# Turning the column order of the MoE matmuls' moving operand and result

## The chip, the cores and the metric

The kernel runs on one core of one Trainium2 chip. The metric is the device time of one execution in microseconds (us). The reported time of a kernel is the median of several executions; the profile is one further execution of its own.

## The reference

The reference has two stages. The first is a set attention over four batches of 12480 tokens with 128 channels: 32 inducing vectors attend to all tokens of their batch, and then every token attends to the 32 vectors that came out. The second is a dense feed-forward layer (called MoE in the code, though it has no routing) on all 49920 tokens.

```python
def mab(q, kv):
    s = scale * (q @ kv.transpose(0, 2, 1))
    s = s - s.max(-1, keepdims=True)
    a = np.exp(s)
    a /= a.sum(-1, keepdims=True) + 1e-09
    return a @ kv
h = mab(I, x)            # 32 vectors per batch
x = mab(x, h)            # 49920 tokens x 128
hidden = x @ w_in        # 128 -> 2048
g = hidden * (1.0 / (1.0 + np.exp(-1.702 * hidden)))
out = g @ w_out          # 2048 -> 128
```

The weights arrive as 64-bit numbers, which the kernel turns into float32 on the chip.

## The kernel before

**Layout.** Channels or hidden units lie on the 128 partitions and tokens along the free axis, so a matmul has a 128x128 block of weights as its stationary operand, 512 tokens as its moving operand, and a 128x512 result in one bank of PSUM. The tokens are worked through in blocks of 512 (some left-over blocks are 384 wide, made of two parts of 192). The hidden layer has 2048 / 128 = 16 chunks; two neighbouring chunks form one step, so a block has 8 steps, and all 98 blocks have 784 steps.

**The first MoE matmul** (`firsts`, the matmul at line 491). The second attention ends in a product with 32 vectors `h`, and the first MoE layer is a product too, so the kernel forms `h @ w_in` once per batch (`hw`) and multiplies the attention weights with it. The 32 weights of each token stand four times above one another in `st`, as a rounded upper part and a rest, against upper part and rest of `hw`; so one matmul with 128 rows gives the product at nearly full precision. Both operands are of the type float32r, a rounded float32 that TensorE takes in one go. The result goes to the two halves `ph[:, 0]` and `ph[:, 1]` of a PSUM tile of two banks; there are two such tiles.

**The activation** (`gelus`, line 515, on ScalarE) reads both halves of `ph` in one instruction and writes `g` in float32. `g` is then split into a rounded part `hi` (either by ScalarE from `ph` a second time, line 531, or by VectorE from `g`, line 538) and a rest `lo = g - hi` (VectorE, line 547).

**The second MoE matmul** (`seconds`, lines 605 to 607) adds three products per chunk into `pso`: `wl` with `hi`, `wh` with `lo`, and `wh` with `hi`, where `wh` and `wl` are the rounded part and the rest of `w_out`. Sixteen chunks make 48 matmuls into one bank, of which the first starts and the last ends the sum. The first 12 steps of the kernel are the exception: there `w_out` is not split yet, and one full float32 matmul per chunk (`whole`, line 591, weights `wf`) takes `g` as it is. A block whose early chunks went that way has its later chunks added by lines 605 to 607 into the same `pso`. When the sum is complete, `out` copies it to `ob` (lines 567 and 570) and SyncE's queue stores it.

**Buffers.** `hi`, `lo`, `st` and `hw` come from `spaced`, which makes each buffer 8 elements longer than its data (`STEP = 8`). There are six buffers each of `hi` and `lo`, three of `g`, two of `ph` and two of `pso`.

**Order.** Nothing is scheduled on the chip. When the program is built, the class `Plan` simulates all engines with a cost for each `Job` and writes out one fixed order of instructions per engine. Its cost for a float32r matmul is `2.5 + 0.447 * w` nanoseconds for `w` columns (lines 497 and 610). The attention of the next batch is woven in between the MoE steps of the current one: its matmuls (lines 300, 308, 319, 821) go to TensorE between MoE matmuls, and its exponentials, transposes and sums to ScalarE and VectorE. TensorE thus has one list of instructions, in which the four turned lines (491, 605, 606, 607) make up most of the entries. Each matmul is preceded by a weight load that shows on its own row of the profile (PEld).

**What waits for what around the changed lines.** Line 491 waits for `st` and `hw` (DMA), and for its `ph` buffer to be read by lines 515 and 531. Lines 605 to 607 wait for `hi` and `lo`, and at the first chunk for the `pso` buffer. Line 515 waits for the second half of `ph`, and line 567 or 570 for the last matmul of a block. All these waits are on whole instructions.

Of the kernel before, what the change touches and what calls it, by code (L numbers as in the profile page):

```python
# [17 lines left out]
P = 128  # L18
# [216 lines left out]
def set_attention_then_moe(ctx: ExitStack, tc, xT, x, indT, w_in, w_out, outT):  # L235
# [211 lines left out]
    def new_st(name):  # L447
        return Unit(NG, parts=G if len(name) == 3 else 2 * RG * G)
# [4 lines left out]
    def tokens(i):  # L453
        return sum(p[2] for p in work[steps[i][0]][1])

    def late(least, most):
        return lambda: most if ahead() >= AHEAD else least
# [16 lines left out]
    def firsts():  # L474
        for i in range(n):
            bi, k = steps[i]
            key, of = work[bi]
            if key not in st_units:
                st_units[key] = new_st(key)
            for b, _, _, _ in of:  # L480
                for c in range(G):
                    h_units.setdefault((b, c), Unit(uses_hw[b], parts=G))
            stu = st_units[key]
            hwu = [h_units[b, 2 * k // 4] for b, _, _, _ in of]

            def emit(i=i, k=k, of=of, stu=stu, hwu=hwu):
                st, ph = stu.ap, phs[i].ap
                for c in range(2):
                    ch = 2 * k + c
                    for (b, at, w, _), u in zip(of, hwu):  # L490
                        pe_.matmul(  # L491
                            ph[:, c, at:at + w], u.ap[:, ch % 4 * P:(ch % 4 + 1) * P],
                            st[:, at:at + w], start=True, stop=True,
                        )
                counts["F"] = i + 1

            one_ = 2.5 + 0.447 * tokens(i)
            yield Job("PE", emit, 2 * one_, 2 * one_ + 200, [stu, *hwu], takes=[(r_ph, phs[i])], rank=(1, i), slack=late(0, 800))
# [63 lines left out]
    def out(bi, pso):  # L562
        w = sum(p[2] for p in work[bi][1])
        ob = Unit(len(work[bi][1]))

        def by_act():
            act.copy(ob.ap[:, 0:w], pso.ap[:, 0:w])  # L567

        def by_dve():
            dve.tensor_copy(ob.ap[:, 0:w], pso.ap[:, 0:w])  # L570

        yield [
            Job("ACT", by_act, *on_act(w), [pso], [], [(r_ob, ob)], rank=(0, bi)),
            Job("DVE", by_dve, *on_dve(w), [pso], [], [(r_ob, ob)], rank=(0, bi)),
        ]
        yield from store(bi, ob)

    def seconds():
        psos = {}
        for i, (bi, k) in enumerate(steps):  # L580
            w = tokens(i)
            if k == 0:
                psos[bi] = Unit(parts=NCH)
            pso = psos[bi]
            for c in range(2):
                ch = 2 * k + c

                join = {"joins": [pso]} if ch else {"takes": [(r_po, pso)]}

                def whole(i=i, c=c, ch=ch, w=w, pso=pso):  # L590
                    pe_.matmul(  # L591
                        pso.ap[:, 0:w], wf[:, ch * P:(ch + 1) * P], gs[i].ap[:, c, 0:w],
                        start=(ch == 0), stop=(ch == NCH - 1),
                    )
                    counts["S"] += 1

                if i < plain:
                    occ = 4 * (1 + 0.4185 * w)
                    yield Job("PE", whole, occ, occ + 200, [gs[i], wf_units[ch // G]], rank=(2, i), **join)
                    continue  # L600

                def emit(i=i, c=c, ch=ch, w=w, pso=pso):
                    o = pso.ap[:, 0:w]
                    hi, lo = his[i].ap[:, c, 0:w], los[i].ap[:, c, 0:w]
                    pe_.matmul(o, wl[:, ch, :], hi, start=(ch == 0), stop=False)  # L605
                    pe_.matmul(o, wh[:, ch, :], lo, start=False, stop=False)  # L606
                    pe_.matmul(o, wh[:, ch, :], hi, start=False, stop=(ch == NCH - 1))  # L607
                    counts["S"] += 1

                occ = 3 * (2.5 + 0.447 * w)  # L610
                yield Job(
                    "PE", emit, occ, occ + 200, [his[i], los[i], w_out_units[ch // G]], rank=(2, i), **join,
                )
            if k == NG - 1:
                plan.spawn(out(bi, pso))
# [1049 lines left out]
```

## Time and profile before

| what | value |
|---|---|
| time, median of 3 executions | 1584.58 us (1583.19 to 1584.76) |
| time of the profiled execution | 1583.06 us |
| span of the profiled execution, first to last instruction | 1581.3 us |
| mean granted TensorE clock | 1.000 |
| TensorE busy | 1566.8 us (99%) |
| weight loads busy | 1222.0 us (77%) |
| VectorE busy | 1336.9 us (85%) |
| ScalarE busy | 1323.7 us (84%) |
| DMA, mean over the span | 79 GB/s |

The span is the part that the profile sees; 1583.06 - 1581.3 = 1.8 us of the execution's own time lie outside it. In a row of the profile the line number is that of the kernel, then come the engine, the operation, the names of output and inputs, the shapes, and the count of instructions; behind the bar stand the busy time in us, the mean duration of one in ns, and the idle time of the engine just before such instructions with what ended it. Matmuls are pipelined: the record of one begins before the record of its predecessor ends, so the duration of one record is longer than its share of the time. The share is read from the distance between the starts of two neighbouring matmuls, called the pitch in what follows. The type in a matmul's row says f32 for float32 and float32r alike.

### The profile page before, as it was taken

Reading aid. Unit: us, or ns where it says so; the run is one execution under the profiler, and the core shown is the slowest. Engines: PE = TensorE matmul, PEld = TensorE weight load, DVE = VectorE, ACT = ScalarE, POOL = GpSimd, SP = SyncE. Lnnn points to the kernel's source line nnn. Section 1 sums busy time; section 2 is a strip of 40 time slices with the busy share of each in tenths; the row PEclk is TensorE's granted clock in tenths of the full one; section 3 lists DMA queues with packets and bytes.
Section 4 is the critical chain, followed back from the end, with each engine's and each line's share of the span. In section 5 each row is a group of like instructions: output and inputs, shape, how many; then the busy total and the mean of one; then the engine's idle time right before and its main releaser. Section 6 shows DMA issues by size and latency. Waiting matters only on the chain.

```text
span 1581.3 us, 21430 instructions
## 1 busy us (share of the span) xinstructions
PE 1566.8 (99%) x7693; PEld 1222.0 (77%) x7693; DVE 1336.9 (85%) x1616; ACT 1323.7 (84%) x1502; POOL 0.7 (0%) x6
## 2 busy tenths in 40 slices
PE   8999999999999999999999999999999999999999
PEld 6467777777877887777777887787788878888887
DVE  6999888888888888879888888798898898888886
ACT  5898888788887888878888888798888888887876
POOL 0000000000000000000000000000000000000000
PEclk9999999999999999999999999999999999999999
DMA  7354253430123406342014427220101101111100
GB/s 270 139 190 87 80 102 80 136 113 28 52 97 125 87 27 124 70 150 93 27 41 146 117 54 142 76 72 27 41 26 42 38 29 42 37 36 32 41 27 21
DMA packets 84474, 125.06 MB, mean 79 GB/s; under 512 B 12113, under 2 KB 51601, under 8 KB 78993
## 3 DMA queue, kind: packets, MB, share of 16 engines
q1 hardware_dynamic: 84368, 123.69, 28.4%
q8 instruction: 62, 1.02, 0.3%
q14 instruction: 44, 0.35, 0.1%
HBM read 70.43 MB, written 25.56 MB: 61 GB/s over the span
## 4 chain that ended last, share of the span: by engine, by line
PE 61%; ACT 0%; issue 0%
PE ph L491 15%; PE pso L605 15%; PE pso L607 15%; PE pso L606 15%; PE pa L308 1%; PE pa L319 1%; PE pa L300 0%; PE pa L821 0%; ACT g L515 0%; ACT e L746 0%; ACT L515 0%; ACT ob L567 0%; PE pa L331 0%; ACT e_last L746 0%; PE pa L332 0%
## 5 line engine op out<-in xcount | busy, mean ns | idle before, releaser
L547 DVE TENSOR_TENSOR lo<-g,hi 128x1024 fp32r<-128x1024 f32 (+1 forms) x772 | 929.8, 1215 | 192.4 <-ACT hi L531 180.8
L515 ACT ACTIVATE g<-ph 128x1024 f32<-128x1024 f32 (+1 forms) x784 | 804.3, 1032 | 220.0 <-PE ph L491 94.0
L605 PE MATMUL pso<-hi,wl 128*128 128x512 f32 (+1 forms) x1544 | 607.8, 394 | 0.0
L606 PE MATMUL pso<-lo,wh 128*128 128x512 f32 (+1 forms) x1544 | 606.6, 393 | 0.5 <-DVE lo L547 0.5
L607 PE MATMUL pso<-hi,wh 128*128 128x512 f32 (+1 forms) x1544 | 606.9, 393 | 0.0
L531 ACT ACTIVATE hi<-ph 128x1024 fp32r<-128x1024 f32 (+1 forms) x460 | 474.6, 1034 | 4.6 <-PE pso L607 4.3
L491 PE MATMUL ph<-st,hw 128*128 128x512 f32 x1536 | 467.5, 400 | 4.1 <-ACT hi L531 1.6
L491 PEld LDWEIGHTS ph<-st,hw 128*128 128x128 f32 x1536 | 282.4, 188 | 97.5 <-ACT g L515 10.8
L605 PEld LDWEIGHTS pso<-hi,wl 128*128 128x128 f32 x1544 | 290.1, 188 | 70.4 <-issue 3.6
L606 PEld LDWEIGHTS pso<-lo,wh 128*128 128x128 f32 x1544 | 290.1, 188 | 67.7 <-DVE lo L547 1.4
L607 PEld LDWEIGHTS pso<-hi,wh 128*128 128x128 f32 x1544 | 290.0, 188 | 66.4
L538 DVE CAST hi<-g 128x1024 fp32r<-128x1024 f32 (+1 forms) x312 | 210.6, 681 | 13.5 <-ACT g L515 9.6
L567 ACT COPY ob<-pso 128x512 f32<-128x512 f32 (+1 forms) x70 | 41.7, 595 | 9.8 <-PE pso L607 9.5
L570 DVE COPY ob<-pso 128x512 f32<-128x512 f32 x28 | 19.2, 684 | 8.0 <-PE pso L607 7.8
L300 PE MATMUL pa<-xt,indT_sb 128*32 128x512 f32 x192 | 23.7, 599 | 1.3 <-DMA xt<-in_xT 1.2
L591 PE MATMUL pso<-g,wf 128*128 128x512 f32 x48 | 23.1, 594 | 0.0
L308 PE MATMUL pa<-xt,hT 128*32 128x512 f32 x184 | 22.9, 599 | 0.0
L319 PEld LDWEIGHTS pa<-xn,t 128*32 128x32 f32 (+1 forms) x594 | 15.6, 110 | 4.4 <-issue 3.6
L319 PE MATMUL pa<-xn,t 128*32 128x128 f32 (+1 forms) x594 | 18.8, 274 | 0.0
L970 DVE TENSOR_TENSOR t<-t,two 128x512 f32<-128x512 f32 (+1 forms) x27 | 16.7, 618 | 1.3 <-ACT two L959 1.0
L871 DVE STREAM_TRANSPOSE e<-pa 128x512 f32<-128x512 f32 x23 | 15.9, 702 | 0.5 <-PE pa L308 0.4
L954 DVE STREAM_TRANSPOSE t<-e 128x512 f32<-128x512 f32 x23 | 16.2, 705 | 0.1
(169 smaller groups left out, 421.2 us busy)
## 6 DMA issues: line engine op xcount, KB each, us to landing
xt<-in_xT SPq DMA_DIRECT2D x42, 1024.0 KB, 6.3
out_T<-ob SPq DMA_DIRECT2D x96, 256.0 KB, 2.0
xn<-in_x SPq DMA_DIRECT2D x72, 256.0 KB, 6.9
st<-two SPq DMA_DIRECT2D x184, 64.0 KB, 2.0
st<-t SPq DMA_DIRECT2D x184, 64.0 KB, 2.0
hw<-t SPq DMA_DIRECT2D x48, 64.0 KB, 3.2
raw<-in_w_in SPq DMA_DIRECT2D x4, 512.0 KB, 6.9
raw<-in_w_out SPq DMA_DIRECT2D x4, 512.0 KB, 5.0
```

Source lines behind the costliest of these rows:

```text
L300: pe_.matmul(pa[32 * j:32 * j + 32, 0:w], indT_sb, xg[:, j], start=True, stop=True)
L308: pe_.matmul(pa[32 * j:32 * j + 32, 0:w], hT[:, 0:M], x[:, j * w:(j + 1) * w], start=True, stop=True,)
L319: pe_.matmul(pa[32 * j:32 * j + 32, 0:P], aT[0:q, kk, :], xn[0:q, kk] if second is None or kk < BLK // 2 else second[0:q, kk - BLK // 2], ...
L491: pe_.matmul(ph[:, c, at:at + w], u.ap[:, ch % 4 * P:(ch % 4 + 1) * P], st[:, at:at + w], start=True, stop=True,)
L515: act.activation(gs[i].ap[:, :, 0:w], phs[i].ap[:, :, 0:w], AF.Gelu_apprx_sigmoid)
L531: act.activation(his[i].ap[:, :, 0:w], phs[i].ap[:, :, 0:w], AF.Gelu_apprx_sigmoid)
L538: dve.tensor_copy(his[i].ap[:, :, 0:w], gs[i].ap[:, :, 0:w])
L547: dve.tensor_sub(los[i].ap[:, :, 0:w], gs[i].ap[:, :, 0:w], his[i].ap[:, :, 0:w].bitcast(F32))
L567: act.copy(ob.ap[:, 0:w], pso.ap[:, 0:w])
L605: pe_.matmul(o, wl[:, ch, :], hi, start=(ch == 0), stop=False)
L606: pe_.matmul(o, wh[:, ch, :], lo, start=False, stop=False)
L607: pe_.matmul(o, wh[:, ch, :], hi, start=False, stop=(ch == NCH - 1))
```

## The change

Line 491 and lines 605 to 607 keep their stationary operands, their order, their tiles and their flags. The moving operand is read from its last column to its first, and the result is written from the last column of its region to the first, so every token's result stands where it stood. The two views are made by `[:, ::-1]`, a step of -1 element along the free axis. The full float32 matmul at line 591, the attention's matmuls, all other engines' instructions and the planner's costs are as before.

```diff
                     for (b, at, w, _), u in zip(of, hwu):
                         pe_.matmul(
-                            ph[:, c, at:at + w], u.ap[:, ch % 4 * P:(ch % 4 + 1) * P],
-                            st[:, at:at + w], start=True, stop=True,
+                            ph[:, c, at:at + w][:, ::-1], u.ap[:, ch % 4 * P:(ch % 4 + 1) * P],
+                            st[:, at:at + w][:, ::-1], start=True, stop=True,
                         )
...
                 def emit(i=i, c=c, ch=ch, w=w, pso=pso):
                     o = pso.ap[:, 0:w]
                     hi, lo = his[i].ap[:, c, 0:w], los[i].ap[:, c, 0:w]
+                    o, hi, lo = o[:, ::-1], hi[:, ::-1], lo[:, ::-1]
                     pe_.matmul(o, wl[:, ch, :], hi, start=(ch == 0), stop=False)
                     pe_.matmul(o, wh[:, ch, :], lo, start=False, stop=False)
                     pe_.matmul(o, wh[:, ch, :], hi, start=False, stop=(ch == NCH - 1))
```

## The prediction

> **What bounds the kernel now.** I read the page's totals and its chain of waits first, then the groups of instructions with different shapes kept apart.
>
> ```profile
> span 1581.3 us, 21430 instructions
> PE 1566.8 (99%) x7693; PEld 1222.0 (77%) x7693; DVE 1336.9 (85%) x1616; ACT 1323.7 (84%) x1502; POOL 0.7 (0%) x6
> PEclk9999999999999999999999999999999999999999
> PE 61%; ACT 0%; issue 0%
> ```
>
> ```profile
> L547 DVE TENSOR_TENSOR lo<-g,hi 128x1024 fp32r<-128x1024 f32 x756 | 914.6, 1221 | 187.6 <-ACT hi L531 176.2 <-PE pso L606 0.9
> L515 ACT ACTIVATE g<-ph 128x1024 f32<-128x1024 f32 x768 | 791.5, 1037 | 214.7 <-PE ph L491 93.2 <-ACT g L515 59.4 <-DVE lo L547 29.6
> L605 PE MATMUL pso<-hi,wl 128*128 128x512 f32 x1512 | 596.9, 395 | 0.0
> L607 PE MATMUL pso<-hi,wh 128*128 128x512 f32 x1512 | 596.1, 394 | 0.0
> L606 PE MATMUL pso<-lo,wh 128*128 128x512 f32 x1512 | 595.8, 394 | 0.5 <-DVE lo L547 0.5
> L491 PE MATMUL ph<-st,hw 128*128 128x512 f32 x1536 | 467.5, 400 | 4.1 <-ACT hi L531 1.6 <-DVE st L1560 1.3 <-ACT g L515 1.1
> L605 PE MATMUL pso<-hi,wl 128*128 128x384 f32 x32 | 10.9, 341 | 0.0
> L491 PE MATMUL ph<-left,hw 128*128 128x192 f32 x64 | 8.8, 270 | 0.0
> ```
>
> TensorE is busy for 1566.8 of 1581.3 us at the full granted clock, the chain that ended last is nearly TensorE alone, and in front of the four changed lines it stood idle for 4.1 + 0.5 us in all. VectorE and ScalarE, in contrast, have 187.6 and 214.7 us of idle time in front of their largest groups. So TensorE is the bound from start to end, and whatever a changed matmul gains or loses counts at once.
>
> A record of 395 ns overlaps its neighbours, so I need the pitch. For it I looked for a long stretch with nothing but the changed lines in it, and took the groups in that stretch and its first and last rows in order of time.
>
> ```profile
> L607 PE MATMUL pso<-hi,wh 128*128 128x512 f32 x110 | 43.4, 395 | 0.0
> L605 PE MATMUL pso<-hi,wl 128*128 128x512 f32 x110 | 43.4, 395 | 0.0
> L606 PE MATMUL pso<-lo,wh 128*128 128x512 f32 x110 | 43.3, 394 | 0.0
> L491 PE MATMUL ph<-st,hw 128*128 128x512 f32 x102 | 29.5, 394 | 0.0
> ```
>
> ```profile
> 504.06 0.50 PE L605 MATMUL pso<-hi,wl 128*128 128x512 f32 x1
> 504.39 0.39 PE L606 MATMUL pso<-lo,wh 128*128 128x512 f32 x1
> ...
> 604.15 0.40 PE L607 MATMUL pso<-hi,wh 128*128 128x512 f32 x1
> ```
>
> That is 110 + 110 + 110 + 102 = 432 matmuls, so 431 distances from 504.06 to 604.15 us: 100.09 / 431 = 0.2322 us for 512 columns. How much of this goes by columns shows in a row of 384-wide ones:
>
> ```profile
> 445.66 0.34 PE L605 MATMUL pso<-hi,wl 128*128 128x384 f32 x1
> ...
> 447.76 0.35 PE L605 MATMUL pso<-hi,wl 128*128 128x384 f32 x1
> ```
>
> Twelve distances (four times lines 605, 606 and 607) lie between these two, 2.10 / 12 = 0.175 us each. (0.2322 - 0.175) / 128 columns = 0.447 ns per column, which leaves 0.2322 - 512 x 0.000447 = 0.003 us that doesn't depend on the width. The time of a changed matmul is a stream of columns, and the change touches just this stream.
>
> **The change part by part.** *Instructions.* None is added, removed or moved: the groups above keep their counts, no DMA is touched, and every wait is on a whole instruction. A consumer (line 515 on `ph`, lines 567 and 570 on `pso`) begins when the last column is written, whichever it is. Cost 0. I also see no danger in mixing orders: a sum that line 591 began in the old order is continued in the new one, but reading and writing are both turned, so each column meets its own place.
>
> *How many columns.* 3 x 1512 + 1536 = 6072 matmuls of 512, 3 x 32 = 96 of 384 and 64 of 192. (96 x 384 + 64 x 192) / 512 = 96, so 6168 matmuls of full width, 6168 x 0.2322 = 1432 us or 91% of the span. Each nanosecond on the pitch is worth 6.2 us.
>
> *Weight loads.* The stationary operand isn't turned. Its loads lie beside the matmuls:
>
> ```profile
> L605 PEld LDWEIGHTS pso<-hi,wl 128*128 128x128 f32 x1544 | 290.1, 188 | 70.4 <-issue 3.6
> ```
>
> 188 ns fit under 232, so they cost nothing now. If the pitch fell, 188 would be the next floor.
>
> *Reading backwards and writing backwards.* No row of this trace has a negative step, so this is the unknown cost, and the two halves can't be priced apart before a run. First the question whether the stream is slowed now by other engines' traffic, which a turned order could meet in another way:
>
> ```profile
> 808.21 0.40 PE L606 MATMUL pso<-lo,wh 128*128 128x512 f32 x1
> 808.23 1.03 ACT L515 ACTIVATE g<-ph 128x1024 f32<-128x1024 f32 x1
> 808.30 1.23 DVE L547 TENSOR_TENSOR lo<-g,hi 128x1024 fp32r<-128x1024 f32 x1
> 808.45 0.40 PE L607 MATMUL pso<-hi,wh 128*128 128x512 f32 x1
> 808.68 0.40 PE L605 MATMUL pso<-hi,wl 128*128 128x512 f32 x1
> ...
> 809.45 0.69 DVE L538 CAST hi<-g 128x1024 fp32r<-128x1024 f32 x1
> 809.85 0.39 PE L605 MATMUL pso<-hi,wl 128*128 128x512 f32 x1
> 810.05 1.03 ACT L515 ACTIVATE g<-ph 128x1024 f32<-128x1024 f32 x1 [0.78 <-PE ph L491]
> 810.08 0.40 PE L606 MATMUL pso<-lo,wh 128*128 128x512 f32 x1
> ```
>
> From 808.45 to 808.68 both other engines are at work, and the pitch is 0.23 us; from 809.85 to 810.05 ScalarE is idle and VectorE runs another operation, and the pitch is 0.23 again. So I find no contention that a new order could relieve or make worse; what sets 0.447 ns per column lies in TensorE's own path.
>
> The two bounds come from the nearest rows of a stream of 512 columns at another rate, the full float32 matmuls of line 591:
>
> ```profile
> L591 PE MATMUL pso<-g,wf 128*128 128x512 f32 x48 | 23.1, 594 | 0.0
> 77.22 1.88 PE L591 MATMUL pso<-g,wf 128*128 128x512 f32 x4
> ```
>
> Four records last 1.88 us together and one alone 0.594, so their pitch is (1.88 - 0.594) / 3 = 0.429 us. This is the dearest stream of that width and the upper bound: 6168 x (0.429 - 0.2322) = +1214 us. If such a record takes its columns through the array twice (48 records stand for 12 steps of two chunks, so each of the 24 calls already makes two), one trip is 0.2145 us, and that is the lower bound: 6168 x (0.2145 - 0.2322) = -109 us. Between ends so far apart I take the row that the turned matmul is nearest to, and that is its own: same engine, type, width, tiles and number of columns per buffer, each column still next to the one before. I take 0.2322, a change of 0.
>
> Here a rule of the Trainium skill speaks against the change. The page "PSUM — Partial Sum Buffer", section "Specifications (TRN2)", gives PSUM lines of 8 bytes and says that any non-contiguous pattern slows matmuls significantly. Whether a step of -1 counts as contiguous it doesn't say; two neighbours in turned order still share a line, and by that reading its sum is the same as mine, while by the strict one it is the second rival below. No row of this trace has a result with any other step than 1, so the trace can't decide it.
>
> *The sum.* 0 (instructions) + 0 (weight loads) + 0 (stream) on 1583.06 us, the profiled execution's own time, of which 1581.3 are its span and 1.8 lie outside. That execution is 1.5 us below the median of the runs shown, 1584.58, so I forecast 1584.5 us. A difference of less than 0.2%, 3.2 us or 0.5 ns on the pitch, I call no change, since this kernel's runs can't tell it.
>
> **The rivals.** *A: the stream gets faster.* For it speaks that 0.2322 isn't the lowest price that a row suggests; something in TensorE's path costs up to 0.018 us per matmul, and if it comes from the order of addresses, turning could remove it. Against it, the trace doesn't show what that is. In full it gives 1583 - 109 = 1474 us. The other engines allow it: in the stretch above their busy times are
>
> ```profile
> 504.05:604.16 100.11, 100.11 (x434) 80.99 (x432) 85.38 (x102) 86.17 (x104) 0.00 (x0) 1.00 0.27 58
> ```
>
> (TensorE, weight loads, VectorE, ScalarE), and 100.11 x 0.2145 / 0.2322 = 92.5 us still hold 85.38 and 86.17. But a fixed order leaves more waits at 93% than at 86%, and I would expect 1475 to 1530.
>
> *B: slower, because columns that come in falling order are no longer taken in pairs.* The place is the access of TensorE to its operand or to PSUM, the price is one column where two went before. It decides from the first matmul, since TensorE has no slack. For it speaks that the cheap rate belongs to rising order in every row that we have; against it, that the rows of line 591 show the array can run at half that rate for reasons of type alone, so their 0.429 proves nothing on addresses. It gives 1583 + 1214 = 2797 us.
>
> *C: some nanoseconds either way.* The records vary from one instruction to the next:
>
> ```profile
> L606 PE MATMUL pso<-lo,wh x110: 387/393/399, 504.4 to 603.9; 128*128 128x512 f32 x110
> ```
>
> The least and the largest lie 6 ns from the median. If start addresses have a part in this, a stream that begins at the other end of the buffer starts in another place; 6 ns each way is 6168 x 0.006 = 37 us, so 1546 to 1621. Against it: with so many buffers in use the mean should move far less than one record does.
>
> *D: the change doesn't do what it says.* If the two turned views were cancelled against each other when the program is built, the same instructions would run, with 1584.5 us.
>
> **How the numbers follow.** Forecast 0.40, D 0.05, A 0.20, B 0.20, C 0.15 (0.06 on the fast side, 0.09 on the slow side, where a stream begun away from its usual end pays first). So faster by over 0.2% has 0.20 + 0.06 = 0.26, no change 0.45, slower 0.20 + 0.09 = 0.29. The likeliest case's own range is 1581 to 1588. The range for 8 in 10 takes in A in full at its low end and C at its upper end, and leaves out B: 1474 to 1621.
>
> **What would show it.** The pitch of lines 491 and 605 to 607 is the whole matter: 0.232 us in a stretch without other lines if I am right, near 0.215 for A, near 0.43 for B, and different means for different lines for C. Line 591 isn't turned, so its pitch must stay 0.43; if it moves too, the cause isn't the order of columns. With A the idle time in front of lines 547 and 515 shrinks from 188 and 215 us, and some appears in front of 491 and 606; with B it grows to many times that, and TensorE stays without gaps. The granted clock should stay at full; if it falls, power rather than addresses has moved the time. The forecast is wrong if the pitch changes by more than 0.5 ns.

## The result and the profile after

The changed kernel takes 1592.82 us (median of 6 executions, 1591.66 to 1593.48) against 1584.59 us before (6 executions, 1583.19 to 1586.15): a ratio of 1.0052, with a 95% interval of 1.0042 to 1.0063. It is slower by 8 us. That is beyond what I called no change, and the forecast was no change; the time lies inside the wide range, but not in the likeliest case's own.

The page of the changed kernel, its totals and its granted clock:

```profile
span 1591.5 us, 21430 instructions
PE 1578.0 (99%) x7693; PEld 1225.6 (77%) x7693; DVE 1338.1 (84%) x1616; ACT 1325.0 (83%) x1502; POOL 0.7 (0%) x6
PEclk9999999999999999999999999999999999999999
```

The counts are those of before, and TensorE is the bound as before: its matmuls became busier by 11.2 us (1566.8 to 1578.0), VectorE and ScalarE by 1.2 and 1.3. The groups with shapes kept apart (lines 605 to 607 are 606 to 608 here, since the change adds a line):

```profile
L547 DVE TENSOR_TENSOR lo<-g,hi 128x1024 fp32r<-128x1024 f32 x756 | 915.1, 1221 | 194.0 <-ACT hi L531 182.8 <-PE pso L607 0.9
L515 ACT ACTIVATE g<-ph 128x1024 f32<-128x1024 f32 x768 | 789.8, 1034 | 222.1 <-PE ph L491 99.4 <-ACT g L515 61.7 <-DVE lo L547 25.3
L606 PE MATMUL pso<-hi,wl 128*128 128x512 f32 x1512 | 601.7, 398 | 0.0
L491 PE MATMUL ph<-st,hw 128*128 128x512 f32 x1536 | 470.9, 403 | 3.8 <-ACT hi L531 1.4 <-DVE st L1561 1.3 <-ACT g L515 0.9
L591 PE MATMUL pso<-g,wf 128*128 128x512 f32 x48 | 23.1, 594 | 0.0
```

VectorE's and ScalarE's instructions last as long as before and wait some 7 us longer (194.0 and 222.1 against 187.6 and 214.7 us): ScalarE's wait for line 491 grew from 93.2 to 99.4 us, and VectorE waits for ScalarE. In front of line 491 there is no more idle time than before, and line 591, which isn't turned, kept its 594 ns. So the time went into the turned matmuls themselves. The stretch of 432 that gave the pitch of before stands in this kernel in the same order; its first and last rows in order of time:

```profile
507.96 0.50 PE L606 MATMUL pso<-hi,wl 128*128 128x512 f32 x1
...
608.84 0.40 PE L608 MATMUL pso<-hi,wh 128*128 128x512 f32 x1
```

100.88 / 431 = 0.2341 us, where it was 0.2322. Over the whole of both traces, the mean distance between two neighbouring turned matmuls of 512 columns (those under 260 ns, some 5900 in each) is 232.01 ns before and 233.64 after. The distances also look different: before, nearly all of them (99.8%) lie between 223 and 243 ns, after between 230 and 241. 6072 x 1.63 ns = 9.9 us, close to the 10.2 us between the two profiled executions (1583.06 and 1593.27) and somewhat more than the 8.2 us between the medians. In the profiled execution of the changed kernel the granted clock was 0.83 between 40 and 50 us, before most of the turned matmuls; the three executions whose mean clock is 1.000 still have a median of 1591.93 us, so this is not the cause.

So the question is why a read in falling order costs 1.6 ns more, if it is the read.

### The profile page after: what moved, and what is told of

The parts are those of the page before. It is cut to its first block, busy times and chain, and to the rows that moved or that the text cites. A ratio compares the mean times of both kernels' runs of the same rounds, so it can differ in the third digit from the quotient of the medians.

```text
span 1591.5 us, 21430 instructions
## 1 busy us (share of the span) xinstructions
PE 1578.0 (99%) x7693; PEld 1225.6 (77%) x7693; DVE 1338.1 (84%) x1616; ACT 1325.0 (83%) x1502; POOL 0.7 (0%) x6
## 4 chain that ended last, share of the span: by engine, by line
PE 61%; ACT 0%; issue 0%
PE ph L491 15%; PE pso L606 15%; PE pso L608 15%; PE pso L607 15%; PE pa L308 1%; PE pa L319 1%; PE pa L300 0%; PE pa L822 0%; ACT g L515 0%; ACT e L747 0%; ACT L515 0%; ACT ob L567 0%; PE pa L331 0%; ACT e_last L747 0%; PE pa L332 0%
## 5 line engine op out<-in xcount | busy, mean ns | idle before, releaser
L515 ACT ACTIVATE g<-ph 128x1024 f32<-128x1024 f32 (+1 forms) x784 | 802.6, 1030 | 227.5 <-PE ph L491 100.2
L567 ACT COPY ob<-pso 128x512 f32<-128x512 f32 (+1 forms) x70 | 41.5, 593 | 10.2 <-PE pso L608 9.7
```

The costliest lines, as they stand in the source:

```text
L515: act.activation(gs[i].ap[:, :, 0:w], phs[i].ap[:, :, 0:w], AF.Gelu_apprx_sigmoid)
```

## The experiments

### Reading or writing, first matmul or second

Four kernels, each one part of the change. With reads alone or writes alone turned, the columns of `g`, `hi` and `lo` stand in falling order in between, and the second matmul puts them right; a left-over block's two parts change places in `ph` for the same reason, and line 591 follows.

```diff
 reads only
-    ph[:, c, at:at + w], ..., st[:, at:at + w]
+    ph[:, c, W - at - w:W - at], ..., st[:, at:at + w][:, ::-1]
+    hi, lo = hi[:, ::-1], lo[:, ::-1]
 writes only
+    ph[:, c, W - at - w:W - at][:, ::-1], ..., st[:, at:at + w]
+    o = o[:, ::-1]
```

Reads only. 

> Only the moving operands are read from the last column to the first; results are written in rising order. The columns of g, hi and lo then stand in falling order, and the second matmul's falling read puts them right; line 591 reads g falling too. The changed kernel's pitch rose from 232.0 to 233.6 ns, 9.9 us over 6072 matmuls. Theory R (the falling read costs it): pitch 233.6 ns, 1592 to 1593 us. Theory W (the falling write costs it): pitch 232.0, 1584 to 1585 us. Theory B (it is the pair of both that matters, for example a fixed cost of any pattern with a negative step): in between or the same as with both, and the two single runs don't add up to the whole.

Writes only. 

> The mirror of the run before: results written falling, operands read rising (line 591 writes falling too). Theory R: pitch 232.0 ns, 1584 to 1585 us. Theory W: 233.6 ns, 1592 to 1593 us. Theory B: as in the run before.

Lines 605 to 607 alone, both ways. 

> Lines 605 to 607 turned in both ways, line 491 as before. If the cost is one per turned matmul whatever its line: three quarters of it, 7.4 of 9.9 us, 1590.5 to 1592 us. If it belongs to the sums in PSUM (line 491 doesn't add), all of it; if it belongs to the passage from turned to unturned matmuls, more than the whole.

Line 491 alone, both ways. 

> Line 491 turned in both ways, lines 605 to 607 as before. One cost per turned matmul: a quarter, 2.5 of 9.9 us, 1586.5 to 1588 us. If it belongs to the sums in PSUM: 1584 to 1585 us.

| kernel | median us | ratio to before, 95% interval |
|---|---|---|
| reads only | 1593.51 | 1.0054 (1.0040 to 1.0068) |
| writes only | 1584.73 | 1.0002 (0.9993 to 1.0011) |
| lines 605 to 607 only | 1591.32 | 1.0042 (1.0029 to 1.0054) |
| line 491 only | 1586.80 | 1.0013 (1.0004 to 1.0022) |

The same stretch of 432 in order of time, first with the reads turned, then with the writes turned:

```profile
508.23 0.50 PE L607 MATMUL pso<-hi,wl 128*128 128x512 f32 x1
...
609.10 0.40 PE L609 MATMUL pso<-hi,wh 128*128 128x512 f32 x1
```

```profile
506.70 0.50 PE L607 MATMUL pso<-hi,wl 128*128 128x512 f32 x1
...
606.79 0.40 PE L609 MATMUL pso<-hi,wh 128*128 128x512 f32 x1
```

100.87 / 431 = 0.2340 us and 100.09 / 431 = 0.2322 us. Theory R holds: the falling read costs all of it, the falling write nothing that these runs can tell. The reads alone cost 9.5 us against the 1584.03 us of before in these runs. The three quarters of the matmuls at lines 605 to 607 cost 7.3 us and the quarter at line 491 cost 2.8; within the intervals that is one price per falling read, whether the result is added to a sum or not.

### Bare streams

To see the price without the kernel around it, I ran kernels that hold nothing but stretches of 48 matmuls of one kind, each kind on a line of its own, with a weight block of its own for each of eight matmuls in turn.

> A kernel of its own that leaves the whole computation out: one stretch after another of 48 matmuls of one kind, three times over, with all other engines idle. Each kind has a line. If the pitch is TensorE's own, rising reads with rising writes give 232 ns at 512 columns here too, and both falling 233.6. Falling read alone and falling write alone show which half costs it: theory R 233.6 and 232.0, theory W 232.0 and 233.6. If the column stream is limited by the bytes that the read brings, 16-bit operands (half the bytes) go near 215 ns and don't notice the order; if by the array or by writing, they stay at 232. A start at another column (1, 2, or falling from 512) shows whether the place in a line matters: some ns or nothing. Zeros as data show whether the data matter: the same 232 if not. A read with a step of 2 or 4 (256 columns) shows whether a line of 16 bytes is what is fetched: 2 nearly free, 4 dearer; a write with a step of 2 (16-bit operands) costs about double if only neighbours are written in pairs.

In order of time, the second of the three turns, where a row is one stretch. The pitch is the distance to the start of the next row, divided by 48.

```profile
239.57 11.24 PE L52 MATMUL o<-xs,wr 128*128 128x512 f32 x48
250.65 11.44 PE L55 MATMUL o<-xs,wr 128*128 128x512 f32 x48
261.93 11.25 PE L58 MATMUL o<-xs,wr 128*128 128x512 f32 x48
273.01 11.44 PE L61 MATMUL o<-xs,wr 128*128 128x512 f32 x48
284.29 11.36 PE L64 MATMUL o<-xz,wr 128*128 128x512 f32 x48
...
340.61 10.54 PE L79 MATMUL o<-xb,wb 128*128 128x512 bf16 x48
350.98 10.52 PE L82 MATMUL o<-xb,wb 128*128 128x512 bf16 x48
...
404.64 11.46 PE L100 MATMUL o<-xs,wr 128*128 128x512 f32 x48
415.94 11.25 PE L103 MATMUL o<-xs,wr 128*128 128x512 f32 x48
427.02 11.24 PE L106 MATMUL o<-xs,wr 128*128 128x512 f32 x48
```

Rising read and rising write (L52) take 11.08 / 48 = 0.2308 us, falling read (L55) 0.2350, falling write (L58) 0.2308, both falling (L61) 0.2350. So the effect is TensorE's own, with every other engine idle. 16-bit operands take 10.37 / 48 = 0.216 us rising (L79), and the falling stretch (L82) is as long as the rising one, 10.52 against 10.54 us: they have neither the surcharge nor its dependence on order. L100 reads groups of four columns in falling order, with the four inside a group rising, and pays the falling price, 0.2354; L103 reads the groups rising and the four inside each falling, and pays the rising price, 0.2308. Four float32r columns are 16 bytes, so it is the order of 16-byte pieces that counts. Zeros as data (L64 rising) gave 0.2331, but on a buffer at another place, so whether the data matter stays open. L106 always loads the same weights and doesn't differ from L52.

Two more stretches bear on the second rival, a result written to every other column (16-bit operands, 256 columns; L94 is the plain one, L91 the stepped one):

```profile
377.88 5.44 PE L94 MATMUL o<-xb,wb 128*128 128x256 bf16 x48
383.16 10.52 PE L91 MATMUL o<-xb,wb 128*128 128x256 bf16 x48
393.33 11.49 PE L97 MATMUL o<-xs,wr 128*128 128x256 f32 x48
```

5.28 / 48 = 0.110 us plain and 10.17 / 48 = 0.212 stepped, about twice as much. The rule of the Trainium skill's page "PSUM — Partial Sum Buffer" ("Specifications (TRN2)") on patterns that aren't contiguous thus holds here for a result with a step of 2; a result with a step of -1 isn't slowed (L58 against L52).

The surprise of this kernel was the stretch that read one buffer again and again (L109): 0.2267 us, lower than any other rising one. Where the columns stand seemed to matter, so I varied the start.

> A second kernel of bare streams, with the computation left out as before. All matmuls of a kind read the same 512 columns, from a start of 0, 1, 2, 4, 8, 12, 16, 24 or 32 elements into the buffer, rising and falling; or they go to and fro between two places 1024 + d elements apart. In the first such kernel, rising reads took 231.0 ns over four buffers and 226.7 on one; falling ones took 231 to 237 by buffer. Theory L (lines in falling order are fetched more slowly in the stream itself): on the same columns falling stays above rising by 4 ns or more at every start, 256 columns cost half the difference of 512, and the distance d makes no difference to it. Theory J (the cost lies at the junction, between where one read ends and the next begins): on the same columns falling equals rising, 227 both, 256 columns have the same difference as 512, and the distance d moves both orders by several ns. Both expect a start off a multiple of four elements to cost one more line.

The second turn again: L47 rises from the aligned start, L50 falls over the same columns, and L53 rises from one element on.

```profile
421.45 11.07 PE L47 MATMUL o<-xs,wr 128*128 128x512 f32 x48
432.36 11.37 PE L50 MATMUL o<-xs,wr 128*128 128x512 f32 x48
443.56 11.53 PE L53 MATMUL o<-xs,wr 128*128 128x512 f32 x48
```

Falling took 233.3 to 233.6 ns from every start that is a multiple of four elements, and equally between any two such places. Rising took 227 at the aligned start, 229 to 234 from other multiples of four, and 237 from one element on. That refuted both theories as they stood: J, because rising and falling differed on the same columns; L, because the rising price is no constant to which falling adds. With 256 columns falling was even the cheaper one (118.6 against 120.0 ns), which neither theory had.

The kernel with equal buffers was on record together with these streams. Taking their result for an effect of the columns' address alone, I then aligned the buffers too:

```diff
-STEP = 8
+STEP = 0
 and for the aligned ones, ahead of all buffers
+    const.tile([P, 8], F32, name="pad")
```

> The kernel before with STEP = 0: buffers of hi, lo, st and hw are not shifted against each other by 32 bytes, so all their starts are equal modulo 2048 bytes. Theory J: every junction is like that of the same columns read again, so the pitch falls from 232.0 towards 227 and the time to about 1584 - 31 = 1553 us. Theory L: the pitch stays at 232 and the time at 1584.

> The changed kernel with STEP = 0. Theory J: its junctions are all alike too, so it has the same pitch as the run before, 227, about 1553 us. Theory L: the falling stream keeps its surcharge of 1.6 ns over the run before, 10 us more than it.

> The kernel before with STEP = 0 and a pad of 32 bytes ahead of the buffers, so that every buffer of hi, lo and st starts at a multiple of 256 bytes; nothing is turned. In the bare streams, rising reads took 227.2 ns where the start was such a multiple and 229 to 234 elsewhere, and falling ones 233.4 from any start that is a multiple of 16 bytes. Theory S (a rising stream's price depends on its start modulo 256 bytes, and the kernel before pays the mean over eight phases): pitch 227.2, 6072 x 4.8 ns = 29 us less, 1553 to 1558 us. Theory M (in the kernel other things blur it, since buffers at such a start were no cheaper there than others): 231 to 232, 1578 to 1586 us.

> The changed kernel on the same aligned buffers. Theory S: a falling stream has one price from any such start, pitch 233.4 and 1591 us as without the pad, so that turning costs 6 ns instead of 1.6 on aligned buffers, some 36 us. Theory M: about 1592 us too, but then only 10 us above the run before.

| kernel | order | median us | ratio to before, 95% interval | mean distance ns |
|---|---|---|---|---|
| no spacing | rising | 1586.88 | 1.0018 (1.0009 to 1.0028) | 232.6 |
| no spacing | falling | 1591.24 | 1.0049 (1.0034 to 1.0064) | 233.5 |
| columns aligned | rising | 1586.80 | 1.0016 (1.0007 to 1.0025) | 232.6 |
| columns aligned | falling | 1593.30 | 1.0056 (1.0042 to 1.0071) | 233.4 |

Neither gained anything (both rising kernels are 2 to 3 us slower than before), and theories J and S fell. The falling price was the same 233.4 to 233.5 ns each time. By the addresses in the built programs, which no trace shows, the weights `wh` and `wl` lie 128 bytes (modulo 256) from the columns in both of these rising kernels, in the one at 96 against 224, in the other at 128 against 0; in the bare streams they had lain at 0 against 0. That was the clue to the next theory, V. A third set of streams, with the columns moved in steps of 16 bytes, was already on record with the aligned kernels to test theory S; a fourth, with the weights moved, was made to test V.

> A third kernel of bare streams, the computation left out. Rising reads of the same 512 columns from every 16 bytes of a 256-byte stretch and from 256, 384, 512, 768 and 1024 bytes; falling ones from four of these; widths of 128 to 448 columns from an aligned start both ways. Theory S: rising 227 at 0 and at every multiple of 256 bytes, 229 to 235 in between, with some pattern in 32, 64 or 128 bytes; falling 233.4 throughout. By the two widths seen so far an aligned rising stream costs 0.419 ns per column and 13 ns once, a falling one 0.448 ns per column and 4 ns once; then 128 columns cost about 66 and 61 ns, and 384 about 174 and 176.

> A fourth kernel of bare streams, the computation left out: the same aligned 512 columns each time, and the weights taken from 0 to 96 elements behind an aligned place, rising and falling; then weights and columns in the order wl hi, wh lo, wh hi of the MoE, with the weights aligned or 128 bytes off; and matmuls with only 64 weight columns. Theory V: rising goes from 227 to 230 or more with the weights' place, falling stays at 233.4 or moves less, and with 64 weight columns (half the load) both come nearer to each other. Theory M: the weights' place changes neither, and the order of the MoE gives 231 or more at both places.

The third set, columns moved and weights at their place: L47 is the aligned start, L59 16 elements behind it, L71 32, L83 48 and L92 60. L134 and L137 are 256 columns wide, rising and falling.

```profile
402.41 11.06 PE L47 MATMUL o<-xs,wr 128*128 128x512 f32 x48
413.30 11.28 PE L50 MATMUL o<-xs,wr 128*128 128x512 f32 x48
...
446.82 11.16 PE L59 MATMUL o<-xs,wr 128*128 128x512 f32 x48
...
491.21 11.32 PE L71 MATMUL o<-xs,wr 128*128 128x512 f32 x48
...
536.00 11.35 PE L83 MATMUL o<-xs,wr 128*128 128x512 f32 x48
...
569.65 11.05 PE L92 MATMUL o<-xs,wr 128*128 128x512 f32 x48
...
701.53 5.94 PE L134 MATMUL o<-xs,wr 128*128 128x256 f32 x48
707.31 5.85 PE L137 MATMUL o<-xs,wr 128*128 128x256 f32 x48
713.00 7.20 PE L140 MATMUL o<-xs,wr 128*128 128x320 f32 x48
```

The fourth set, weights moved and columns at their place: L65 4 elements, L77 16, L89 32 and L95 48, all rising; L50 is falling with aligned weights. L119 and L125 rise in the order of the MoE (`wl` with `hi`, `wh` with `lo`, `wh` with `hi`), with the weights aligned and 32 elements off.

```profile
432.93 11.37 PE L65 MATMUL o<-xs,wr 128*128 128x512 f32 x48
...
477.75 11.36 PE L77 MATMUL o<-xs,wr 128*128 128x512 f32 x48
...
522.60 11.31 PE L89 MATMUL o<-xs,wr 128*128 128x512 f32 x48
...
545.10 11.16 PE L95 MATMUL o<-xs,wr 128*128 128x512 f32 x48
...
634.33 11.06 PE L119 MATMUL o<-xs,wr 128*128 128x512 f32 x48
...
656.43 11.32 PE L125 MATMUL o<-xs,wr 128*128 128x512 f32 x48
...
723.14 11.37 PE L50 MATMUL o<-xs,wr 128*128 128x512 f32 x48
```

All rows have 48 matmuls, so the durations of those 512 wide can be compared directly (the pitch is the duration less one record of 0.39 us, over 47). Columns 16 elements on (11.16) cost what weights 48 on cost (11.16), columns 32 on (11.32) what weights 32 on cost (11.31), columns 48 on (11.35) what weights 16 on cost (11.36). 64 elements are 256 bytes, so in these three pairs moving the weights forward is the same as moving the columns back, modulo 256 bytes, and three more pairs of moves by a multiple of eight elements agree as well. The rising price is lowest, 226.7 to 227.5 ns, where the two start alike, and mostly 229 to 234.5 elsewhere. One pair does not fit: columns 60 elements on took 226.8 ns (L92), as little as an aligned start, while weights 4 on, which should be the same, took 233.5 (L65). So the distance between the two starts is not the whole rule. Falling (L50) is 233.4 at nearly every place, and the order of the MoE gives 227.0 ns rising with the weights aligned and 232.5 with them 128 bytes off, close to the 232.6 that the kernel with aligned columns had paid.

The surcharge of the falling read belongs to the width, too: at 256 columns it is -1.9 ns (5.78 / 48 = 120.4 rising, 5.69 / 48 = 118.5 falling), at 320 none, at 384 +3.6, and only at 512 the 6.4 seen above. At 128 and 192 columns each matmul with its load takes 111 to 112 ns in either order, not the 61 to 66 that I had expected for 128.

The Trainium skill's page "TensorE: Matmul & The Clock Gate", Part 2, step 1, gives TensorE two independent read ports and says that loading the next weights takes no bandwidth from the running matmul. These rows speak against it for float32r: the same columns, read in the same order, take 0.227 or 0.233 us by nothing but the place of the weights that are loaded beside them, while the record of such a load stays at 187 to 189 ns.

### The kernel with weights and columns aligned

```diff
-STEP = 8
+STEP = 0
+    const.tile([P, 40], F32, name="pad")     ahead of wh and wl
+    const.tile([P, 32], F32, name="pad2")    behind wl
```

> As the kernel with the aligned buffers, and the weights wh and wl at multiples of 256 bytes too (they lay 128 bytes off; hw was aligned already). In the bare streams, where the rising pitch was 227, the weights were aligned. Theory V (the weights that are loaded beside the stream have a part in the price, by their place): pitch 227 to 229, 1555 to 1567 us. Theory M (in the kernel the price is blurred by the passage between many buffers): 232.5 and 1587 us, like the two kernels without spacing before.

It took 1560.05 us, a ratio of 0.9848 (0.9832 to 0.9865), and Theory V holds. Its stretch of 432 in order of time:

```profile
501.20 0.50 PE L607 MATMUL pso<-hi,wl 128*128 128x512 f32 x1
...
599.22 0.39 PE L609 MATMUL pso<-hi,wh 128*128 128x512 f32 x1
```

98.02 / 431 = 0.2274 us, the price of the bare streams. By the mean distance (227.3 ns against 232.0) 6072 matmuls should save 28 us; 23.5 arrived. Part of the difference is waiting: the distances between turned matmuls that are 260 ns or longer, apart from stretches at a lower granted clock, hold 16.5 us beyond the pitch here and 12.6 before.

Then the change once more, on top of this:

> The kernel with all operands aligned, with the change on top. If the price is set by how the falling or rising stream stands to the weight load read beside it: falling 233.4 ns, 6.1 ns above the rising 227.3, so 6072 x 6.1 = 37 us more than the aligned kernel, about 1595 us, and the same change that cost 8 us on the buffers as they were costs over four times that here. If the change costs something of its own, whatever the places: 1.6 ns or 10 us more, about 1570 us.

```profile
506.65 0.50 PE L608 MATMUL pso<-hi,wl 128*128 128x512 f32 x1
...
607.32 0.40 PE L610 MATMUL pso<-hi,wh 128*128 128x512 f32 x1
```

100.67 / 431 = 0.2336 us, and 1591.06 us in all (ratio to before 1.0043, 1.0026 to 1.0059). That is 31 us more than the aligned kernel, not the 37 that I had expected, but far from the 10 of a fixed surcharge. The same edit that cost 8 us costs 31 us here, and both kernels with it end within 2 us of one another: for these layouts, turning doesn't add a price, it replaces the rising price of a layout by one of 233.4 to 233.6 ns.

Last, the planner was told the new price.

> The kernel with all operands aligned, rising, and the planner's cost of a float32r matmul set to the measured pitch: 2.5 + 0.4391 w instead of 2.5 + 0.447 w (227.3 ns at 512). The fixed orders change a little. If the waits of TensorE that are new in the aligned kernel (about 5 us more in front of line 491 and 607) come from an order made for slower matmuls, 1555 to 1559 us; if not, 1560 as without.

1555.08 us, a ratio of 0.9813 (0.9798 to 0.9827), faster than both kernels. Of the 5.0 us gained over the aligned kernel, the waits in the long distances account for 3.1 (16.5 down to 13.4 us) and the pitch for 0.8 (227.34 to 227.21 ns); where the rest comes from was not looked into.

## Why the prediction was wrong, point by point

*The bound* was right: TensorE alone. That whatever a matmul gains or loses counts at once held for the loss, but not in full for a gain: of the 28 us that aligning took off the pitch, 23.5 arrived. The way to the number, pitch times 6168, was right; with the measured 1.6 ns it gives 10 us, and 8 were measured.

*Instructions, waits, mixed orders, the write*: 0, and writes alone turned measured 1.0002 (0.9993 to 1.0011).

*The step that failed* is the price of the falling read, where I took the turned matmul's own row, 0.2322, for it, "a change of 0"; measured, it is 1.6 ns per matmul of 512 columns, with the write at nothing. Two steps ahead of it led there. The first is "Weight loads": I saw that 188 ns fit under 232 and concluded "so they cost nothing now". Lying beside a matmul isn't the same as being free. The streams with the weights moved show that the same matmul takes 227 to 234 ns by the place of the weights alone. Nor is 188 ns "the next floor": the streams of 256 columns, each with a load of its own, ran at 120 ns with load records of 188 to 192. The second is the search for contention: I compared stretches with VectorE and ScalarE busy and idle, found the same pitch, and went from "no contention" with these to a price of TensorE's own path that order can't touch. The first half holds (the bare streams run at the same prices with all other engines idle); but TensorE's own matmuls and weight loads lie beside one another in time, and that pair I never compared.

*The per-column rate.* I split 0.2322 into 0.447 ns per column and 0.003 us once. On aligned bare streams 256 columns take 120.4 ns, 384 take 174.1 and 512 take 227.0, so 0.416 ns per column and 14 ns once. Falling, they take 118.5, 177.7 and 233.4, so 0.449 and 4. The prediction's split is close to the falling one. What I read as a stream rate was probably a mean over places; that the 14 ns come from the one load per matmul is a guess.

*The rivals.* C had the right mechanism in one half, that places count, and I bounded it well by the 387/393/399 ns of the records; but I held that the mean over many buffers would hardly move. It moved by 1.6 ns. The likely reason is that the kernel's buffers, shifted by 32 bytes each, give rising reads a mean over places and falling reads nearly one price (233.4 to 233.6): the eight rising starts 32 bytes apart in the third set have a mean of 232.0, the pitch of before. That is argued, since no run moves one buffer at a time. A was wrong as to turning, but right that up to 0.018 us per matmul lay there: 0.005 of it could be had, by alignment. B is refuted: falling reads and writes stay within 4% of the rising rate, and only a step of 2 halves it. D is refuted by the result itself.

*The signs to look for* served: the pitch rose by more than 0.5 ns, line 591 did not move, and no wait appeared. The granted clock fell only in the short stretch named above.

**What stays open.** How the two reads meet inside TensorE was not observed; that they collide is argued from the dependence on places, and columns 60 elements on (226.8 ns) do not fit a rule of the distance alone. Nor does a matmul's own pair of places decide its distance alone: a stream that reads the same aligned columns rising and falling in turn took 236.5 ns, more than either order by itself, and neighbours at line 491, whose own operands `st` and `hw` were aligned in both by the built programs, took 231.0 ns in the kernel with only its columns aligned and 227.5 once `wh` and `wl` were moved as well. The falling price isn't quite one number: with weights 128 bytes off, the bare streams in the order of the MoE took 240.0 ns falling and one at 32 elements 236.6, while the kernel with only its columns aligned, whose `wh` and `wl` are 128 bytes off as well, took 233.4. And a matmul with 64 weight columns, whose load is shorter (134 against 188 ns), took 230.0 rising and 233.4 falling, no less than one with 128 (227.0 and 233.4), which a plain count of collisions would not give.

## What to carry to other kernels

A matmul's pitch in a long stretch should be compared with the best pitch that the same shape reaches anywhere, not only with itself under other engines' load; 232 against 227 ns was worth 1.5% of this kernel, and 1.9% with the planner told of it. With float32r operands 512 columns wide, it is worth trying to let moving and stationary operands start at the same place modulo 256 bytes, weights included: aligning the columns alone gained nothing. An edit whose price depends on the layout around it, as the turned read did (8 us on one layout, 31 on another), has no price of its own that could be carried over.

## What the runs showed of the hardware that I had not expected

- The pitch of float32r matmuls with 512 columns depends on where columns and weights start: rising 226.7 to 227.5 ns where the two are alike modulo 256 bytes and up to 234.5 from other multiples of four elements, falling near 233.4, on an otherwise idle core. With 256 columns falling is the cheaper order (118.5 against 120.4). 16-bit operands take 216 ns both ways.
- What counts as falling is the order of 16-byte pieces (0.2354 us); turning the four columns inside a piece costs nothing (0.2308).
- Reading every other float32r column makes 256 columns cost 228 ns, against 121 for neighbours, almost as much as all 512 would; reading every fourth costs 236, hardly more than every other.
